# A dynamic convolution feeding a tanh-shrink MLP: the first x tile of a batch in one DMA, and another tap order for superblock 4

## The chip, the cores and the metric

The kernel runs on one core of one Trainium2 chip. The metric is the device time of one execution in microseconds (us); lower is better. The kernel before takes 751.6 us, the median of four runs (750.75 to 754.11). A core has five engines that run beside each other and wait for each other through semaphores: TensorE (PE, with its weight loads shown apart as PEld), VectorE (DVE), ScalarE (ACT), GpSimd (POOL) and SyncE (SP), which here only issues DMAs. Sixteen DMA engines move the data of all queues.

## What is computed

Eight batches of 4096 positions, 192 channels in 8 heads of 24. For each position and head a softmax over 7 taps gives weights; the output is the weighted sum of the 7 latest rows of x, zeros standing ahead of a batch's first row. That goes through a two-layer MLP with the activation h - tanh(h):

```python
def attn(x, weight_gen):
    w = softmax(weight_gen, axis=-1)              # [B, S, 8, 7]
    x_pad = concat([zeros(B, 6, 192), x], axis=1)
    out[b, s, h, g] = sum_k w[b, s, h, k] * x_pad[b, s + k, h, g]
    ...
h = out.reshape(32768, 192) @ w_in                # 192 x 2048
y = (h - tanh(h)) @ w_out                         # 2048 x 192
```

## The kernel before

The 32,768 tokens are cut into 32 superblocks of 1024. A batch has four, so superblocks 0, 4, 8, ... 28 are the first of a batch. On chip, each of the 128 partitions holds 8 consecutive tokens (J = 8). An x tile has 6 halo rows (the six tokens before the partition's own) and 8 rows: 14 rows of 192 floats, 10.5 KB per partition. Partition 0 of a batch's first tile has zeros in its halo rows.

For a superblock n the work passes through these stages.

1. SP loads the x tile (`load_x`, L110 to L150) and the tap weights (`load_wg`). Two x tiles exist. The load of tile n + 1 is tied by a dependency to the first product of superblock n (`x_after`, L280).
2. ScalarE takes the exponential of the weights, VectorE sums, inverts and scales.
3. `products` (from L229): GpSimd multiplies x rows by tap weights, giving seven bf16 product tensors: taps 0 to 3 in a tile `pa`, taps 4 to 6 in a tile `pb` that has a single buffer. For superblocks listed in HELP (4 to 31), one row of taps 0 and 1 is made by VectorE instead (L289). Product tensors are then partly summed by an accumulating DMA that GpSimd issues (`dma_sum`, L221). There are three ways: superblocks in PART add taps 2 and 3 onto 0 and 1 before the `pb` product is made, so five tensors remain; the others add the three of `pb` onto taps 0 to 2, so four remain; TWO_SUMS (13 on) add again, so two remain.
4. `conv_sums` (L338): PE transposes the remaining tensors against an identity matrix and sums them in PSUM; for each tensor 24 small matmuls, 16 for chunks 0 and 1 and 8 for chunk 2. ScalarE copies the result out as convT.
5. `gemm1` (L381) multiplies by one of 16 blocks (f) of w_in, ScalarE takes tanh (L394), VectorE subtracts (L395).
6. `out_pairs` (L417) multiplies by w_out, ScalarE copies out (L436), and SP stores (L440).

The order on each engine is the order in which the program is written. In the main loop, iteration n runs the 16 f steps of superblock n. In the same iteration stand: the products of superblock n + 2 (from f = 1, their second part at f = 3), the transposes of superblock n + 1 (chunks 0 and 1 at f = 13, chunk 2 at f = 14), the second matmul of superblock n - 1 and n spread as pairs over all f steps, and the loads of x tile n + 3 at f = 1 (at f = 9 in iteration 1). SP's queue therefore mixes x loads, weight loads and output stores in that order, and each waits its turn.

A batch's first x tile, except that of superblock 0, takes four DMAs: 112 partitions in full, rows without the halo for the first 16 partitions, the halo for partitions 1 to 15, and zeros for partition 0.

Of the kernel before, what the change touches and what calls it, by code (L numbers as in the profile page):

```python
# [16 lines left out]
def kernel(  # L17
# [8 lines left out]
    nc = tc.nc  # L26
# [15 lines left out]
    NFT = F // P  # L42
    NC = D // R
    KA, KH = 4, 2
    PART = (2, 3, 4)
    TWO_SUMS = (13, 14, 15, 16, 17, 18, 19, 20, 21, 22, 23, 24, 25, 26, 27, 28, 29, 30, 31)
    AHEAD = 4
    STORE_FIRST = 8
    EXTRA = (5, 9, 11, 13)
    HELP = (4, 5, 6, 7, 8, 9, 10, 11, 12, 13, 14, 15, 16, 17, 18, 19, 20, 21, 22, 23, 24, 25, 26, 27, 28, 29, 30, 31)  # L50
    HELP_AT = 3
    SCALE_TWICE = True
    assert S % TOK == 0 and D % R == 0 and F % P == 0
    assert NFT == 2 * J, "one token block of the second matmul per pair of f tiles"

# [14 lines left out]
    make_identity(nc, ident[:])  # L70

    obank = [psum_o.tile([P, 512], FP32, name=f"obank{i}", tag=f"obank{i}") for i in range(2)]
    zero = const.tile([1, D], FP32, name="zero")
    nc.vector.memzero(zero[:])
    once = const.tile([P, 1], FP32, name="once")
# [15 lines left out]
    last_conv = {}  # L91
    first_halo = {}
    x_after = {}

    def order(inst, other, reason):
        tc.add_manual_dep(
# [16 lines left out]
    def load_x(n, behind=None):  # L113
        b, s = divmod(n, NSB)
        s0 = s * TOK

        x_t = xpool.tile([P, HALO + J, D], FP32, name="x_t")

        def rows(p0, p1, r0=0, r1=HALO + J):
            first = x[0, 0:1]  # L120
            return nc.sync.dma_start(
                out=x_t[p0:p1, r0:r1, :],
                in_=bass.AP(
                    tensor=first.tensor,
                    offset=first.offset + (b * S + s0 + p0 * J - HALO + r0) * D,
                    ap=[[J * D, p1 - p0], [D, r1 - r0], [1, D]],
                ),
            )

        def no_halo():  # L130
            nc.sync.dma_start(
                out=x_t[0:1, 0:HALO, :],
                in_=zero[:].rearrange("o (h d) -> o h d", h=1).to_broadcast([1, HALO, D]),
            )


        if n == 0:
            rows(0, P, HALO, HALO + J)
            rows(16, P, 0, HALO)
            rows(1, 16, 0, HALO)  # L140
            no_halo()
        else:
            dma = rows(16 if s == 0 else 0, P)
            if behind is not None:
                order(dma, behind, "order of the loads")
            if s == 0:
                rows(0, 16, HALO)
                rows(1, 16, 0, HALO)
                no_halo()
        x_of[n] = x_t  # L150

    def softmax_exp(n):
# [75 lines left out]
    def products(n, taps=None, sums=None, hooks={}):  # L228

        x_t = x_of.pop(n)  # L230
        wsm, wsm_v, e_t, zr = wsm_of.pop(n)
        if e_t is not None:
            scale(nc.gpsimd, wsm[:], e_t, zr[:])

        pa = papool.tile([P, KA, J, D], BF16, name="pa")
        if n == 1:

            last = [opool.tile([P, 2, J, D], BF16, name="pb1", tag="out_sb") for _ in range(2)]
            home = [(pa, 0, KA), (last[0], KA, KA + 2), (last[1], KA + 2, K)]
        else:  # L240
            pb = pbpool.tile([P, K - KA, J, D], BF16, name="pb")
            home = [(pa, 0, KA), (pb, KA, K)]
        x_v = x_t[:]
        step = x_v.ap[0]

        def prod(k0, k1):
            for t, a, b in home:
                if a <= k0 and k1 <= b:
                    return t[:, k0 - a : k1 - a]

        def mul(eng, k0, k1, j0=0, j1=J):

            w = wsm_v if eng is nc.vector else wsm[:]
            nj = j1 - j0
            return eng.tensor_mul(  # L255
                prod(k0, k1)[:, :, j0:j1].rearrange("p k j (h g) -> p k (j h) g", h=H),
                bass.AP(
                    tensor=x_v.tensor,
                    offset=x_v.offset + (k0 + j0) * D,
                    ap=[step, [D, k1 - k0], [G, nj * H], [1, G]],  # L260
                ),
                w[:, j0:j1]
                .rearrange("p j h (k o) -> p k (j h) o", o=1)[:, k0:k1]
                .to_broadcast([P, k1 - k0, nj * H, G]),
            )

        def parts(*ks):
            return [[prod(k, k + 1)[:, 0] for k in ks]] * NC

        if taps is not None:  # L270
            for eng, k0, k1, j0, j1 in taps:
                m = mul(eng, k0, k1, j0, j1)
                if j1 == 1:
                    first_halo[0] = m
                if k0 in hooks:
                    hooks[k0]()
            prods_of[n] = parts(*sums)
            return

        x_after[n + 1] = mul(nc.gpsimd, 0, KH, 0, J - 1 if n in HELP else J)  # L280
        mul(nc.gpsimd, KH, KA)
        second_sum(n - 1)

        def rest(ph=None):
            if n in HELP:

                w = ph[:, 0, 0 : KH * H].rearrange("p (k h) -> p k h", k=KH)
                nc.vector.tensor_copy(w, wsm[:, J - 1].rearrange("p h k -> p k h")[:, 0:KH])
                nc.vector.tensor_mul(  # L289
                    pa[:, 0:KH, J - 1, :].rearrange("p k (h g) -> p k h g", h=H),  # L290
                    bass.AP(
                        tensor=x_v.tensor,
                        offset=x_v.offset + (J - 1) * D,
                        ap=[step, [D, KH], [G, H], [1, G]],
                    ),
                    w.rearrange("p k (h o) -> p k h o", o=1).to_broadcast([P, KH, H, G]),
                )
            if n in PART:
                dma_sum(pa[:, 0:2], pa[:, 2:4])
            mul(nc.gpsimd, KA, K)  # L300
            if n in PART:
                prods_of[n] = parts(4, 5, 6, 0, 1)
            else:
                dma_sum(pa[:, 0:3], pb[:, 0:3])
                if n in TWO_SUMS:
                    to_sum[n] = pa
                    prods_of[n] = parts(0, 1)
                else:
                    prods_of[n] = parts(3, 0, 1, 2)
                if n == NTOT - 1:  # L310
                    second_sum(n)

        return rest
# [62 lines left out]
    def gemm1(n, f):  # L376
        convT = conv_of[n]
        ph = psum_h.tile([P, 2, HT], FP32, name="ph", tag="ph")
        for c in range(NC):
            for r in range(2):  # L380
                nc.tensor.matmul(  # L381
                    ph[:, r, :],
                    lhsT=w_in[r * R : (r + 1) * R, c, f * P : (f + 1) * P],
                    rhs=convT[r * R : (r + 1) * R, c, :],
                    start=(c == 0),
                    stop=(c == NC - 1),
                )
        th = tpool.tile([P, TOK], FP32, name="th")
        ph_f = ph[:].rearrange("p r t -> p (r t)")
        gt = gpool.tile([P, TOK], BF16, name=f"gt{f}", tag=f"gt{f}")  # L390
        if n == 1 and f == 2:

            probe[0] = nc.scalar.activation(out=once[:], in_=ph_f[:, 0:1], func=ACT.Copy)
        last_act[0] = nc.scalar.activation(out=th[:], in_=ph_f, func=ACT.Tanh)  # L394
        last_sub[0] = nc.vector.tensor_sub(gt[:], ph_f, th[:])  # L395
        g_of.setdefault(n, []).append(gt)
        return ph

    LAST = (NTOT - 1) * J
    half = {}  # L400
# [162 lines left out]

    EARLY, THIRD = ((7, 3), (9, 1), (11, 7)), 13
    for f in range(NFT):
        gemm1(0, f)
        if f == 1:
            softmax_exp(3)
        if f == EARLY[0][0]:
            pcs = []  # L570
            sums = conv_sums(1, ((0, 1),), pcs, obank)
        for at, groups in EARLY:
            if f == at:
                some(sums, groups * PER)
        if f == EARLY[-1][0]:
            conv_out(1, ((0, 1),), pcs)
        if f == THIRD:
            pcs = []
            for _ in conv_sums(1, ((2,),), pcs, obank):
                pass  # L580
            conv_out(1, ((2,),), pcs)

    STEADY = dict(pairs=(5, 11, 0, 16, 4, 12, 6, 10, 0, 6, 10, 8, 8, 8, 8, 16), t1=(14, 8), t2=(13, 0), scale=14, sums=(1, 13))
    FIRST = dict(pairs=(4, 12, 0, 16, 1, 15, 0, 16, 0, 16, 0, 13, 3, 0, 16, 16), t1=(15, 2), t2=(11, 10), scale=15, sums=(1, 2, 3, 4, 8, 10))


    def transposes(n, chunks):
        pcs = []  # L590
# [16 lines left out]
    for n in range(1, NTOT):  # L607
        more = n < NTOT - 1
        finish = []
        plan = FIRST if n == 1 else STEADY  # L610

        soft = [m for m in (n + 3 if n <= AHEAD else n + 4,) if m < NTOT]
        for f in range(NFT):
# [42 lines left out]
            if f >= plan["scale"]:  # L656
                for scale_one in finish:
                    scale_one()
                finish = []
            out_pairs(plan["pairs"][f] - done)  # L660
            if f == (9 if n == 1 else 1) and n <= STORE_FIRST:
                loads(n)
# [36 lines left out]
```

## Time and profile before

| what | us |
|---|---|
| median of the runs | 751.6 |
| profiled execution, its run | 750.75 |
| its span in the profile | 749.0 |
| PE busy on the second matmul (L417) | 410.8 |
| PE busy on the first matmul (L381) | 419.9 |
| PE busy on transposes from pa / pb (L338) | 40.2 / 6.3 |
| one subtraction on DVE (L395) | 1.218 |
| one tanh on ACT (L394) | 1.026 |
| GpSimd product 128x4608 / 128x3072 / 128x2688 | 9.07 / 6.02 / 5.42 |
| sum pa<-pb, issue to landing (least, median, most) | 8.8, 9.5, 11.2 |
| x tile in one DMA, issue to landing, median | 7.7 |
| x tile's part of 112 partitions, the same | 9.2 |

Busy times of different engines lie beside each other, so they are not added. The matmuls of PE overlap each other as well. GpSimd's durations are means over the whole run[...]. The granted PE clock is full except at a few places. A superblock takes PE about 22.4 us in the first third and 21.8 us later, when fewer tensors are transposed.

### The profile page before, as it was taken

The numbers are of one execution on the slowest core, as the hardware profiler recorded it, in microseconds if no ns is written. First come the engines' busy times: TensorE is split into PE (matmuls) and PEld (weight loads), VectorE is DVE, ScalarE is ACT, GpSimd is POOL, SyncE is SP. The second block draws the span as 40 slices with busy tenths as digits, with TensorE's granted clock in tenths as the row PEclk, the third lists the DMA queues.
The fourth block names the chain that finished last, engine by engine and source line by source line (L and its number), as shares of the span: only waits on it lengthen the run. The fifth ranks groups of instructions, "written<-read, shape, count | busy, mean of one in ns | idle before, by whom it ended". The sixth has DMA issues, their size and how long they took to land.

```text
span 749.0 us, 30081 instructions
## 1 busy us (share of the span) xinstructions
PE 722.9 (97%) x13640; PEld 559.8 (75%) x13640; DVE 684.2 (91%) x711; ACT 639.9 (85%) x872; POOL 657.9 (88%) x158
## 2 busy tenths in 40 slices
PE   3899999999999989999999999999999999999997
PEld 2477777777777777777777777787777777877777
DVE  7999999989999979999999999999999999988893
ACT  4888888888888868888989989888998989888882
POOL 7999999999999999999999999999999999992000
PEclk9899999999999999999999999999999999999999
DMA  8926536865667659887779878787988877776112
GB/s 234 243 46 159 173 116 178 192 174 133 171 162 177 178 170 222 179 214 175 195 206 224 207 199 202 173 197 205 230 192 193 211 176 190 195 148 110 45 44 86
DMA packets 34464, 129.64 MB, mean 173 GB/s; under 512 B 4808, under 2 KB 9656, under 8 KB 30480
## 3 DMA queue, kind: packets, MB, share of 16 engines
q0 software_dynamic: 19296, 50.73, 39.4%
q1 hardware_dynamic: 15040, 77.00, 29.1%
q8 instruction: 106, 1.74, 0.9%
q14 instruction: 22, 0.18, 0.1%
HBM read 54.49 MB, written 25.17 MB: 106 GB/s over the span
## 4 chain that ended last, share of the span: by engine, by line
PE 93%; DVE 3%; issue 1%; DMA 1%; ACT 1%; DVEq 0%
PE obank L417 44%; PE ph L381 44%; PE pc L338 4%; PE po L460 1%; DVE gt L395 1%; DMA x_t<-in_x_dram 1%; ACT th L394 1%; DMA wg_t<-in_weight_gen_dram 0%; DVE pa L255 0%; DVE pb L255 0%; DVE wsm L214 0%; DVE zsum L168 0%; ACT wg_t L154 0%; DVE obank L196 0%; ACT convT L356 0%
## 5 line engine op out<-in xcount | busy, mean ns | idle before, releaser
L395 DVE TENSOR_TENSOR gt<-ph,th 128x1024 bf16<-128x1024 f32 x512 | 602.0, 1218 | 40.9 <-ACT th L394 27.8
L394 ACT ACTIVATE th<-ph 128x1024 f32<-128x1024 f32 x512 | 514.0, 1026 | 70.7 <-PE ph L381 62.4
L381 PE MATMUL ph<-convT,w_in 64*128 64x512 bf16 x3072 | 419.9, 379 | 5.0 <-DVE gt L395 3.5
L417 PEld LDWEIGHTS <-gt 64*128 64x128 bf16 x7936 | 357.7, 94 | 87.9 <-issue 14.0
L417 PE MATMUL obank<-w_out,gt 64*128 64x192 bf16 x7936 | 410.8, 243 | 6.0 <-issue 5.6
L255 POOL TENSOR_TENSOR pa<-x_t,wsm 128x3072 bf16<-128x3072 f32 (+2 forms) x63 | 341.6, 5655 | 0.2
L255 POOL TENSOR_TENSOR pb<-x_t,wsm 128x4608 bf16<-128x4608 f32 (+2 forms) x33 | 283.6, 8595 | 0.7 <-DMA x_t<-in_x_dram 0.4
L381 PEld LDWEIGHTS <-w_in 64*128 64x128 bf16 x3072 | 164.5, 95 | 79.8 <-issue 18.5
L436 ACT ACTIVATE out_sb<-obank 128x192 f32<-128x192 f32 x248 | 81.2, 328 | 15.4 <-PE obank L417 15.0
L364 ACT ACTIVATE convT<-pc 128x1024 bf16<-128x1024 f32 (+1 forms) x62 | 50.2, 811 | 1.2 <-PE pc L338 0.7
L221 POOL DMA_DIRECT2D pa<-pb x27 | 34.7, 1284 | 15.2 <-DVE pa L289 8.3
L338 PEld LDWEIGHTS <-pa 64*128 64x128 bf16 x2016 | 40.9, 100 | 7.2 <-POOL pa L255 1.1
L221 POOL DMA_DIRECT2D pa<-pa x22 | 35.4, 1607 | 8.7 <-DMA pa<-pb 7.8
L338 PE MATMUL pc<-ident,pa 64*128 64x64 bf16 x1920 | 40.2, 191 | 1.6 <-POOL pa L255 0.9
L168 DVE TENSOR_REDUCE zsum<-wg_t 128x32 f32<-128x224 f32 (+1 forms) x61 | 23.6, 387 | 3.0 <-ACT wg_t L154 3.0
L154 ACT ACTIVATE wg_t<-wg_t 128x448 f32<-128x448 f32 x32 | 18.2, 570 | 6.9 <-DMA wg_t<-in_weight_gen_dram 6.9
L214 DVE TENSOR_TENSOR wsm<-wg_t,pc 128x448 f32<-128x448 f32 x27 | 16.8, 621 | 3.0 <-DVE pc L183 0.5
L289 DVE TENSOR_TENSOR pa<-x_t,ph 128x384 bf16<-128x384 f32 x28 | 15.5, 554 | 1.2
L183 DVE RECIPROCAL pc<-zsum 128x64 f32<-128x64 f32 x27 | 14.9, 550 | 1.6 <-ACT convT L364 1.6
L338 PE MATMUL pc<-ident,pb 64*128 64x64 bf16 x288 | 6.3, 202 | 9.2 <-POOL pb L255 9.2
L338 PEld LDWEIGHTS <-pb 64*128 64x128 bf16 x360 | 7.7, 105 | 9.9 <-POOL pb L255 9.1
L460 PE MATMUL po<-w_out,gt 64*128 64x192 bf16 x256 | 11.2, 243 | 0.0
(27 smaller groups left out, 55.6 us busy)
## 6 DMA issues: line engine op xcount, KB each, us to landing
x_t<-in_x_dram SPq DMA_DIRECT2D x24, 1344.0 KB, 7.7
pa<-pb POOLq DMA_DIRECT2D x27, 1152.0 KB, 9.5
out_dram<-out_sb SPq DMA_DIRECT2D x31, 768.0 KB, 4.5
pa<-pa POOLq DMA_DIRECT2D x22, 768.0 KB, 7.5
x_t<-in_x_dram SPq DMA_DIRECT2D x7, 1176.0 KB, 9.2
wg_t<-in_weight_gen_dram SPq DMA_DIRECT2D x32, 224.0 KB, 7.3
x_t<-in_x_dram SPq DMA_DIRECT2D x1, 768.0 KB
w_out<-in_moe_w_out_dram POOLq DMA_DIRECT2D x1, 768.0 KB, 9.4
```

Source lines behind the costliest of these rows:

```text
L154: last_exp[0] = nc.scalar.activation(out=wg_t[:].rearrange("p j h k -> p (j h k)"), in_=wg_t[:].rearrange("p j h k -> p (j h k)"), func=AC ...
L168: nc.vector.reduce_sum(out=zsum_of[n][:, j0 * H : j1 * H], in_=e_of[n][:, j0:j1].rearrange("p j h k -> p (j h) k"), axis=AX.X,)
L221: return nc.gpsimd.dma_start(out=out.rearrange("p k j d -> p k (j d)"), in_=in_.rearrange("p k j d -> p k (j d)"), accum_op=mybir.AluOpTyp ...
L255: return eng.tensor_mul(prod(k0, k1)[:, :, j0:j1].rearrange("p k j (h g) -> p k (j h) g", h=H), bass.AP(tensor=x_v.tensor, offset=x_v.offs ...
L338: nc.tensor.matmul(pc[r][:, col : col + R] if home else pc[:, r, col : col + R], lhsT=prods[c][gi][r * R : (r + 1) * R, 2 * j : 2 * j + 2] ...
L364: last_conv[0] = nc.scalar.activation(out=out, in_=pc[:, :, 0:cols].rearrange("p r (cj t) -> p r cj t", t=R), func=ACT.Copy,)
L381: nc.tensor.matmul(ph[:, r, :], lhsT=w_in[r * R : (r + 1) * R, c, f * P : (f + 1) * P], rhs=convT[r * R : (r + 1) * R, c, :], start=(c == ...
L394: last_act[0] = nc.scalar.activation(out=th[:], in_=ph_f, func=ACT.Tanh)
L395: last_sub[0] = nc.vector.tensor_sub(gt[:], ph_f, th[:])
L417: mm = nc.tensor.matmul(po[:, 0:D], lhsT=g_of[n][f][r * R : (r + 1) * R, col : col + P], rhs=w_out[r * R : (r + 1) * R, f, :], start=(r == ...
L436: last_act[0] = nc.scalar.activation(out=out_sb[:, j, :], in_=po[:, 0:D], func=ACT.Copy)
L460: nc.tensor.matmul(po[:, r, 0:D], lhsT=g_of[n][f][r * R : (r + 1) * R, col : col + P], rhs=w_out[r * R : (r + 1) * R, f, :], start=(f == 0 ...
```

## The change

Superblock 4 leaves PART, so its taps 4 to 6 are summed by DMA onto taps 0 to 2. It is also in a new list, LAST_TAP: GpSimd makes taps 0 and 1, tap 2, then taps 4 to 6, issues the sum, and makes tap 3, which is not summed, last. PE's conv of superblock 4 now reads the four tensors 3, 0, 1, 2 in place of 4, 5, 6, 0, 1.

The first x tile of the batches 1 to 7 (superblocks 4, 8, ... 28) is loaded with one DMA over all partitions. For partition 0 this reads the last six rows of the previous batch into the halo. Zeros are written over them by a small DMA that is issued later, in iteration n - 3 at f = 8 (at f = 10 for superblock 4), and has to wait for the load to land.

Other new names (RELIEF, X_LATE, APART, gemm1_relieved) are empty or not reached.

```diff
-    PART = (2, 3, 4)
+    PART = (2, 3)
+    LAST_TAP = (4,)
+    X_LATE = ()
+    ZERO_AT = 8
...
-            dma = rows(16 if s == 0 else 0, P)
+            dma = rows(16 if s == 0 and ZERO_AT is None else 0, P)
             if behind is not None:
                 order(dma, behind, "order of the loads")
-            if s == 0:
+            if s == 0 and ZERO_AT is None:
                 rows(0, 16, HALO)
                 rows(1, 16, 0, HALO)
                 no_halo()
+            elif s == 0:
+                halo_of[n] = no_halo
...
-        x_after[n + 1] = mul(nc.gpsimd, 0, KH, 0, J - 1 if n in HELP else J)
-        mul(nc.gpsimd, KH, KA)
-        second_sum(n - 1)
+        first = mul(nc.gpsimd, 0, KH, 0, J - 1 if n in HELP else J)
+        if n in LAST_TAP:
+
+            x_after[n + 1] = mul(nc.gpsimd, KH, KA - 1)
+            second_sum(n - 1)
+        else:
+            mul(nc.gpsimd, KH, KA)
+            second_sum(n - 1)
+        if n not in LAST_TAP or n not in X_LATE:
+            x_after[n + 1] = first
...
                 dma_sum(pa[:, 0:3], pb[:, 0:3])
+                if n in LAST_TAP:
+                    mul(nc.gpsimd, KA - 1, KA)
...
+            if n + 3 in halo_of and f >= ZERO_AT:
+
+                halo_of.pop(n + 3)()
             out_pairs(plan["pairs"][f] - done)
```

More of the change, by code (lines that the diff above doesn't have):

```diff
@@ L50 @@
     HELP = (4, 5, 6, 7, 8, 9, 10, 11, 12, 13, 14, 15, 16, 17, 18, 19, 20, 21, 22, 23, 24, 25, 26, 27, 28, 29, 30, 31)
+    LAST_TAP = (4,)
+    X_LATE = ()
+    ZERO_AT = 8
     HELP_AT = 3
     SCALE_TWICE = True
+    RELIEF = ()
     assert S % TOK == 0 and D % R == 0 and F % P == 0
@@ L72 @@
     obank = [psum_o.tile([P, 512], FP32, name=f"obank{i}", tag=f"obank{i}") for i in range(2)]
+    if RELIEF:
+        minus = const.tile([P, P], FP32, name="minus")
+        nc.gpsimd.tensor_scalar_mul(minus[:], ident[:], -1.0)
     zero = const.tile([1, D], FP32, name="zero")
@@ L93 @@
     x_after = {}
+    halo_of = {}
     def order(inst, other, reason):
@@ L397, in gemm1, with gemm1_relieved, subtract, evict @@
         return ph
+    def gemm1_relieved(n, f):
+        convT = conv_of[n]
+        for c in range(NC):
+            for r in range(2):
+                nc.tensor.matmul(
+                    obank[r][:],
+                    lhsT=w_in[r * R : (r + 1) * R, c, f * P : (f + 1) * P],
+                    rhs=convT[r * R : (r + 1) * R, c, :],
+                    start=(c == 0),
+                    stop=(c == NC - 1),
+                )
+        th = tpool.tile([P, TOK], FP32, name="th")
+        gt = gpool.tile([P, TOK], BF16, name=f"gt{f}", tag=f"gt{f}")
+        for r in range(2):
+            nc.scalar.activation(out=th[:, r * HT : (r + 1) * HT], in_=obank[r][:], func=ACT.Tanh)
+        g_of.setdefault(n, []).append(gt)
+        def subtract():
+            for r in range(2):
+                nc.tensor.matmul(
+                    obank[r][:], lhsT=minus[:], rhs=th[:, r * HT : (r + 1) * HT], start=False, stop=True
+                )
+        def evict():
+            for r in range(2):
+                nc.scalar.activation(out=gt[:, r * HT : (r + 1) * HT], in_=obank[r][:], func=ACT.Copy)
+        return subtract, evict
     LAST = (NTOT - 1) * J
@@ L565 @@
     for f in range(NFT):
-        gemm1(0, f)
+        if f in RELIEF:
+            relieved = gemm1_relieved(0, f)
+        else:
+            gemm1(0, f)
+        for lag, step in ((1, 0), (2, 1)):
+            if f - lag in RELIEF:
+                relieved[step]()
         if f == 1:
@@ L581 @@
             conv_out(1, ((2,),), pcs)
+        out_pairs(dict(()).get(f, 0))
     STEADY = dict(pairs=(5, 11, 0, 16, 4, 12, 6, 10, 0, 6, 10, 8, 8, 8, 8, 16), t1=(14, 8), t2=(13, 0), scale=14, sums=(1, 13))
     FIRST = dict(pairs=(4, 12, 0, 16, 1, 15, 0, 16, 0, 16, 0, 13, 3, 0, 16, 16), t1=(15, 2), t2=(11, 10), scale=15, sums=(1, 2, 3, 4, 8, 10))
+    APART = dict(pairs=(4, 12, 0, 16, 0, 16, 4, 12, 0, 16, 4, 12, 0, 6, 10, 16), t1=(15, 5), t2=(10, 2), scale=15, sums=(7, 10))
+    APART_IN = ()
     def transposes(n, chunks):
@@ L609 @@
         finish = []
-        plan = FIRST if n == 1 else STEADY
+        plan = FIRST if n == 1 else APART if n in APART_IN else STEADY
         soft = [m for m in (n + 3 if n <= AHEAD else n + 4,) if m < NTOT]
```

## The prediction

> **What bounds the kernel now.** I read the page, then who waited for whom on PE after the start-up, then PE in order of time around its gaps, then DMA and clock in those stretches, last GpSimd around superblock 4.
>
> ```profile
> PE 722.9 (97%) x13640; PEld 559.8 (75%) x13640; DVE 684.2 (91%) x711; ACT 639.9 (85%) x872; POOL 657.9 (88%) x158
> ...
> q8 instruction: 106, 1.74, 0.9%
> ...
> PE 93%; DVE 3%; issue 1%; DMA 1%; ACT 1%; DVEq 0%
> ```
>
> The chain is TensorE work for 93%, so nothing counts unless it takes work from PE or idle time from it. The waits of PE between 40 and 740 us are a single row (waiting line, releaser, us in total, times, longest):
>
> ```profile
> PE obank L417 <- issue: 5.6, 5, 2.8
> ```
>
> So no GpSimd product, x load or sum holds PE up by name after the start-up: 5.6 us in five gaps for which no semaphore answers. The two large ones, in order of time (start, us, engine and line, idle before it):
>
> ```profile
> 149.55 0.74 PE L417 MATMUL obank<-w_out,gt 64*128 64x192 bf16 x13
> 152.15 0.32 PE L417 MATMUL obank<-w_out,gt 64*128 64x192 bf16 x3 [1.86 <-issue]
> ...
> 265.77 1.05 PE L417 MATMUL obank<-w_out,gt 64*128 64x192 bf16 x20
> 269.60 0.67 PE L417 MATMUL obank<-w_out,gt 64*128 64x192 bf16 x6 [2.79 <-issue]
> ```
>
> The stretches of the second (PE, PEld, DVE, ACT, POOL busy, then granted clock, DMA share, GB/s):
>
> ```profile
> 266.50:269.60 3.10, 0.32 (x8) 0.10 (x4) 2.11 (x3) 0.41 (x1) 3.10 (x2) 0.91 0.98 374
> 269.60:271.50 1.90, 1.90 (x15) 1.45 (x16) 0.00 (x0) 0.33 (x1) 1.90 (x2) 0.50 0.60 234
> ```
>
> PE stops in the middle of a group, and after the second gap it runs 1.9 us at clock 0.50. Counting PE's recorded instructions, the gaps stand before numbers 5313 and 9921, two smaller ones (0.46 at 318.7, 0.28 at 494.2) before 11713 and 18113: every distance is a multiple of 256. Queue q8 has 106 packets of 16.4 KB (1.74 MB / 106), and 27,280 matmuls and weight loads make 106.6 blocks of 256. They are instruction fetches that came late. From the packet records of q8, a fetch starts when PE enters a block, needs about 1 us, and PE goes on 1.5 us after its end (150.61 to 152.14; 268.11 to 269.60). A fetch asked for while a sum or load already stands in the DMA engines comes behind it: those of the two gaps were asked for at about 145 and 262 and served at 149.49 and 267.16. What stood before the first, and the same with an undivided x tile:
>
> ```profile
> DMA packets 376, 1.66 MB, mean 225 GB/s; under 512 B 85, under 2 KB 219, under 8 KB 263
> ...
> DMA packets 315, 1.65 MB, mean 285 GB/s; under 512 B 48, under 2 KB 176, under 8 KB 186
> ```
>
> 143.0 to 150.4 (x tile of superblock 8 in four pieces, its weights, the end of a sum) against 122.0 to 127.8 (superblock 7, one piece): equal bytes, 7.4 against 5.8 us. Last, GpSimd:
>
> ```profile
> 73.82 10.97 POOL L255 TENSOR_TENSOR pa<-x_t,wsm 128x2688 bf16<-128x2688 f32 x2
> 85.08 1.20 POOL L221 DMA_DIRECT2D pa<-pa  x1 [0.30 <-POOL pa L255]
> 85.86 8.80 POOL L255 TENSOR_TENSOR pb<-x_t,wsm 128x4608 bf16<-128x4608 f32 x1
> 94.17 10.96 POOL L255 TENSOR_TENSOR pa<-x_t,wsm 128x2688 bf16<-128x2688 f32 x2
> ```
>
> Superblocks 4 to 12 follow each other every 20.4 us without a wait, while PE takes 22.4: the sums' times do not depend on PE there.
>
> [...]
>
> **The change part by part.**
>
> *Fewer taps in the conv of superblock 4.* Five groups become four: 24 matmuls and 24 weight loads less. Chunks 0 and 1 took 101.47 to 102.63 (1.16 us, 80 matmuls), those of superblock 5 with four groups 124.81 to 125.74 (0.93); a third chunk in proportion 0.12. Gain 0.35 us, on PE.
>
> *GpSimd's order.* The first product stays (73.82 to 79.25). The second, 5.6 us, is cut into two of 2.9 (the row of 128x1536). The pb product moves ahead of the sum and would start at 82.2, but its single buffer is read by the conv of superblock 3 until 82.28: 82.4. It ends at 90.75, the sum is issued at 91.05, the last tap ends at 94.8. Superblock 5 starts at 94.82 instead of 94.17: all sums to superblock 12 come 0.65 us later. GpSimd has 2 us a superblock to spare, so this costs nothing by itself.
>
> *The new wait.* The sum of superblock 4 now carries three taps and is issued 6 us later. Such sums land 9.0 to 11.2 us after issue; with no x load beside it I take 9.3: 100.4. PE comes to that conv at 101.47, does the unsummed tap first (0.23) and needs the sum at 101.7: 1.3 us to spare, at worst (11.2) 0.6 us lost. Queued behind it are the matmuls of f = 13 and all after. I take nothing. Superblock 5 lands at 114.57 + 10.2 = 124.8, needed at 124.7: 0.1 us lost.
>
> *x tiles.* Seven tiles (4, 8, ... 28) lose two DMAs each; the issue falls from 2.0 to 0.33 us on SP. The zeros wait on SP for the tile: out_dram stores and the next x load stand behind them. Tile 4: landing 58.9 + 7.7 = 66.6, so the store of 64.98 goes at about 67.5; its buffer is wanted 20 us later. Tile 12: zeros at about 231, products at 238. Tiles 16 to 28: the zeros stand behind the store (319.56), products start at 325.43[...]. VectorE's own help product does not read the halo. Cost nothing, at worst 1 us on GpSimd, whose sums are 10 us early.
>
> *Instruction fetches.* The 48 missing instructions put every later block boundary 48 instructions later in the work, 0.35 to 1.8 us by where it falls. First gap: x tile 8 starts 0.65 later but is done about 1.6 us earlier; by superblock 7's fetch (3.4 to 4.7 us after the sum's end) it starts at 148.4 instead of 149.5, PE goes on at 151.0, where it would arrive at 150.3: 0.7 lost instead of 2.1. Then two fetches pin PE again: the one behind x tile 9 (PE resumes at 171.7, would reach this at 172.74 in the old timing: at most 1.0 us ahead), the one behind the sum of superblock 11 (248.8 against 249.36: at most 0.55). The one behind sum 12 lets PE go on at 270.25, with 48 more instructions done; the old kernel reached that point at 272.14. So 1.9 us ahead if the clock stays up, 0.6 if it halves again (the gap would be 2.84 us). I take 1.9, this includes all gains so far. Later, sums follow PE. The gaps of 318.7 and 494.2 lie behind the halo tiles 16 and 24 (308.40, 484.24), whose bursts shorten by 1.6 us: their 0.7 us of matmul time goes. New meetings: with boundaries 48 instructions on, those at 328.2, 503.6 and 678.9 fall 2.9 to 3.6 us after a sum's issue; a fetch is then done 10.8 us after it, the next boundary comes at 9.3 to 9.6: from nothing (a fetch just before the sum's packets, 1.85 us after issue) to 1.3 us each. I take nothing for them; all three are in the range.
>
> Sum: 1.9 + 0.7 = 2.6 us less than the profiled execution, whose run took 750.75 us around a span of 749.0. That run was the fastest of four; against the median of 751.6 I keep the difference: 749.0.
>
> **The rivals.** (a) *Faster, as above*: 749.0, chance 0.46; its own range 747.5 to 749.3. (b) *A gain that is pinned*: the clock halves again after 266 (1.3 us lost) and the new meetings cost about 1: 2.6 - 2.3 = 0.3 us, 751.3, within 0.3% (2.25 us, about what a measurement can tell from no change). For it: sums and loads keep their times whatever PE gains. Chance 0.38. (c) *Slower*: the shifted boundaries meet sums. Without the gain at 266, three new gaps of 1.3 us, 1.0 more behind sum 11, one of them long enough for the half clock (1.3): 6.2 - 1.4 (0.35 and the shorter burst) - 0.7 = 4.1, 755.7. It decides once more than 2.25 us of new gaps outlast the gains; against it, the four requests would all have to fall behind the sum's first packets. Chance 0.12. (d) *The second gap goes*: if PE is 1.9 us ahead at 240, the fetches of sums 11 and 12 are asked for before their packets: 2.8 + 1.3 + 2.1 + 0.35 less: 745.1; chance 0.04.
>
> **How the numbers follow.** Faster by over 0.3%: a and d, 0.50; within: 0.38; slower 0.12. The range 745.0 to 752.8 takes a, b, and d, and leaves out c and a tail of b.
>
> **What would show it.** Right: no PE gap of over 1 us near 150, sums from superblock 5 about 0.65 later, PE at the conv of superblock 12 ahead by 1 to 2 us, no gap at the halo tiles. Wrong: a wait of PE for the sum of superblock 4, GpSimd waiting for zeros, or new gaps at distances of 256 from 328, 504, 679. A time over 752.8 would say that the blocks' places, not the length of the bursts, decide.

## The result and the profile after

The changed kernel takes 748.12 us (median of 42 runs), the kernel before 751.31 us in the 63 runs measured beside it: a ratio of 0.995, 95% interval 0.9939 to 0.9961. That is 3.2 us less where 2.6 was forecast. The profiled executions stand 750.75 to 747.22 us, their spans 749.0 to 745.5.

The page of the changed kernel. Labels have moved: L357 is the conv, L400 the first matmul, L466 the second, L231 the summing DMA, L265 the products.

```profile
PE 720.4 (97%) x13616; PEld 555.8 (75%) x13616; DVE 684.2 (92%) x711; ACT 639.2 (86%) x872; POOL 658.1 (88%) x159
...
q8 instruction: 106, 1.74, 0.9%
...
PE 87%; DVE 4%; POOL 3%; DMA 2%; issue 2%; ACT 1%; SPq 0%; DVEq 0%; POOLq 0%
```

Still PE, still 106 instruction fetches. What has changed is in the waits of PE between 40 and 740 us (waiting line, releaser, us in total, times, longest):

```profile
PE obank L466 <- issue: 2.4, 4, 1.2
PE pc L357 <- issue: 1.3, 1, 1.3
PE pc L357 <- DMA pa<-pb: 0.6, 1, 0.6
PE ph L400 <- DVE pa L306: 0.2, 1, 0.2
```

The 5.6 us of unexplained stops have become 3.7, and a wait for a sum has come in. The gap near 150 us is gone. In order of time around the three large ones that are there now (start, us, engine and line, idle before it):

```profile
124.16 0.42 PE L357 MATMUL pc<-ident,pa 64*128 64x64 bf16 x16
125.19 0.88 PE L357 MATMUL pc<-ident,pa 64*128 64x64 bf16 x48 [0.61 <-DMA pa<-pb]
...
266.07 0.57 PE L466 MATMUL obank<-w_out,gt 64*128 64x192 bf16 x9
267.84 0.24 PE L466 MATMUL obank<-w_out,gt 64*128 64x192 bf16 x1 [1.19 <-issue]
...
286.84 0.48 PE L357 MATMUL pc<-ident,pa 64*128 64x64 bf16 x21
288.67 0.33 PE L357 MATMUL pc<-ident,pa 64*128 64x64 bf16 x11 [1.35 <-issue]
```

The stop at 266 us is 1.2 us where it was 2.8 (idle time), and the clock behind it stays whole, where it fell to 0.50 before. The stretches there (busy of PE, PEld, DVE, ACT, POOL, then granted clock, DMA share, GB/s):

```profile
266.00:268.00 2.00, 0.81 (x16) 0.57 (x13) 1.81 (x3) 1.02 (x1) 2.00 (x1) 1.00 1.08 284
268.00:270.00 2.00, 2.00 (x35) 1.71 (x33) 0.75 (x2) 1.24 (x2) 2.00 (x2) 1.00 1.00 391
```

The stop of 1.35 us at 287 is new: the kernel before ran 282 to 292 us without one. To see where time came from and went back, I follow PE through the same work in both traces, by the number of PE instructions done (less the 48 that are missing after superblock 4):

| same point of the work, at us before | after minus before | what lies between |
|---|---|---|
| 99.1 | -0.30 | start |
| 147.9 | +0.15 | fewer taps, then 0.80 lost at the conv of superblock 5 |
| 153.4 | -1.88 | first gap gone |
| 264.6 | -1.56 | small losses, no stop over 0.5 |
| 282.2 | -4.55 | second gap 1.43 in place of 3.03 from start to start, no half clock |
| 312.8 | -3.02 | new gap of 1.54 at 287 |
| 386.8 | -2.47 | gaps of 0.57 at 331 and 0.91 at 379 |
| 744.2 | -3.17 | nothing large |

So the change has gained 4.55 us by 282 us, and 1.4 of it is given back.

GpSimd around superblock 4 (same columns as PE):

```profile
73.67 8.24 POOL L265 TENSOR_TENSOR pa<-x_t,wsm 128x2688 bf16<-128x2688 f32 x2
82.14 8.35 POOL L265 TENSOR_TENSOR pb<-x_t,wsm 128x4608 bf16<-128x4608 f32 x1 [0.22 <-PE pc L357]
90.78 1.28 POOL L231 DMA_DIRECT2D pa<-pb  x1 [0.30 <-POOL pb L265]
91.60 13.86 POOL L265 TENSOR_TENSOR pa<-x_t,wsm 128x1536 bf16<-128x1536 f32 x3
```

The last row runs the unsummed tap of superblock 4 into the two products of superblock 5. The sum of superblock 4, issued at 90.78, had no one waiting for it at 101.4.

Last, the DMA view of 138 to 155 us, x tile 8 among it (queue: packets, MB, share of 16 engines), before:

```profile
DMA packets 669, 2.58 MB, mean 152 GB/s; under 512 B 85, under 2 KB 219, under 8 KB 555
...
q1 hardware_dynamic: 346, 1.61, 36.5%
```

and after:

```profile
DMA packets 633, 2.62 MB, mean 154 GB/s; under 512 B 54, under 2 KB 188, under 8 KB 502
...
q1 hardware_dynamic: 300, 1.61, 23.7%
```

The load queue moves the same 1.61 MB in both (the x tile and the tap weights); 46 packets fewer take a third less time of the DMA engines: 6.2 us of all sixteen against 4.0 (share times 17 us).

### The profile page after: what moved, and what is told of

It is laid out like the page before. It is cut to its first block, busy times and chain, and to the rows that moved or that the text cites. A ratio compares the mean times of both kernels' runs of the same rounds, so it can differ in the third digit from the quotient of the medians.

```text
span 745.5 us, 30018 instructions
## 1 busy us (share of the span) xinstructions
PE 720.4 (97%) x13616; PEld 555.8 (75%) x13616; DVE 684.2 (92%) x711; ACT 639.2 (86%) x872; POOL 658.1 (88%) x159
## 3 DMA queue, kind: packets, MB, share of 16 engines
q8 instruction: 106, 1.74, 0.9%
## 4 chain that ended last, share of the span: by engine, by line
PE 87%; DVE 4%; POOL 3%; DMA 2%; issue 2%; ACT 1%; SPq 0%; DVEq 0%; POOLq 0%
PE ph L400 41%; PE obank L466 41%; PE pc L357 4%; DVE gt L414 2%; POOL pb L265 2%; DMA pa<-pb 1%; PE po L509 1%; POOL pa L265 1%; DMA wg_t<-in_weight_gen_dram 1%; DVE pa L265 1%; ACT th L413 1%; DVE zsum L178 0%; ACT convT L375 0%; SPq L129 0%; DVE obank L206 0%
## 5 line engine op out<-in xcount | busy, mean ns | idle before, releaser
L400 PE MATMUL ph<-convT,w_in 64*128 64x512 bf16 x3072 | 417.4, 378 | 5.8 <-DVE gt L414 4.0
L466 PEld LDWEIGHTS <-gt 64*128 64x128 bf16 x7936 | 355.7, 94 | 83.3 <-issue 7.8
L466 PE MATMUL obank<-w_out,gt 64*128 64x192 bf16 x7936 | 408.1, 243 | 2.6 <-issue 2.4
L265 POOL TENSOR_TENSOR pa<-x_t,wsm 128x2688 bf16<-128x2688 f32 (+2 forms) x64 | 341.9, 5579 | 0.2
L265 POOL TENSOR_TENSOR pb<-x_t,wsm 128x4608 bf16<-128x4608 f32 (+2 forms) x33 | 283.3, 8587 | 0.9 <-ACT wsm L216 0.5
L400 PEld LDWEIGHTS <-w_in 64*128 64x128 bf16 x3072 | 161.2, 94 | 83.1 <-issue 17.9
L357 PEld LDWEIGHTS <-pa 64*128 64x128 bf16 x2064 | 41.8, 100 | 9.6 <-issue 1.8
L231 POOL DMA_DIRECT2D pa<-pb x28 | 36.0, 1284 | 12.0 <-POOL pb L265 9.1
L357 PE MATMUL pc<-ident,pa 64*128 64x64 bf16 x1968 | 40.9, 191 | 3.9 <-issue 1.3
L231 POOL DMA_DIRECT2D pa<-pa x21 | 34.6, 1650 | 9.2 <-DMA pa<-pb 8.6
L193 DVE RECIPROCAL pc<-zsum 128x64 f32<-128x64 f32 x27 | 14.9, 551 | 1.0 <-ACT convT L383 1.0
L357 PE MATMUL pc<-ident,pb 64*128 64x64 bf16 x216 | 4.9, 206 | 9.0 <-POOL pb L265 9.0
L357 PEld LDWEIGHTS <-pb 64*128 64x128 bf16 x288 | 6.3, 107 | 9.5 <-POOL pb L265 9.0
```

What stands on the lines that cost most here:

```text
L231: return nc.gpsimd.dma_start(out=out.rearrange("p k j d -> p k (j d)"), in_=in_.rearrange("p k j d -> p k (j d)"), accum_op=mybir.AluOpTyp ...
L265: return eng.tensor_mul(prod(k0, k1)[:, :, j0:j1].rearrange("p k j (h g) -> p k (j h) g", h=H), bass.AP(tensor=x_v.tensor, offset=x_v.offs ...
L357: nc.tensor.matmul(pc[r][:, col : col + R] if home else pc[:, r, col : col + R], lhsT=prods[c][gi][r * R : (r + 1) * R, 2 * j : 2 * j + 2] ...
L400: nc.tensor.matmul(ph[:, r, :], lhsT=w_in[r * R : (r + 1) * R, c, f * P : (f + 1) * P], rhs=convT[r * R : (r + 1) * R, c, :], start=(c == ...
L466: mm = nc.tensor.matmul(po[:, 0:D], lhsT=g_of[n][f][r * R : (r + 1) * R, col : col + P], rhs=w_out[r * R : (r + 1) * R, f, :], start=(r == ...
```

## The experiments

Three theories. **Burst**: the single x load shortens the burst in front of the fetch, removes the first gap, and the lead gained there softens the second. **Place**: it is the 48 missing instructions, which move every block boundary. **Taps**: the order of the taps in superblock 4 matters by itself. In the expectations below, "theory F" is the first of these (late instruction fetches set the gain), "rival W" says that only PE's own work counts, and "rival D" that the x loads count.

**1. Each part alone.** Starting from the changed kernel, one run leaves the x loads in pieces, the other leaves superblock 4 as it was.

```diff
-    ZERO_AT = 8
+    ZERO_AT = None          # e1_taps_only
...
-    PART = (2, 3)
-    LAST_TAP = (4,)
+    PART = (2, 3, 4)        # e2_one_dma_only
+    LAST_TAP = ()
```

> The tap part of the change alone; first tiles of a batch still come in four DMAs. Theory F (late instruction fetches set the gain): 0.35 us of matmuls less, block boundaries 48 instructions later as in the changed kernel, but long bursts behind the first tiles; the gap near 150 us keeps some 1 to 2 us, the one near 266 us may shrink. 0.5 to 2.5 us less than before, ratio 0.997 to 0.999. Rival W (only the work counts): 0.35 us less, ratio 0.9995. Rival D (the x loads are the gain): no difference.

> The single x load with late zeros alone; superblock 4 as before, so all block boundaries stay at the instructions of the kernel before. Theory F: the gap near 150 us falls from 2.1 to 0.5 to 1 us, PE is then pinned by the late fetch near 266 us, which stays; 0.5 to 1.5 us less, ratio 0.998 to 0.9995. Rival D: nearly the whole gain, 3 us or more less, ratio 0.996 or below. Rival W: no difference.

Taps alone: 749.0 us, ratio 0.9975 (0.9961 to 0.9988), as expected. One DMA alone: 747.66 us, 0.9956 (0.9935 to 0.9977), as good as both together. Here the expectation failed: theory F had the fetch near 266 us pin PE and gave 0.998 to 0.9995, and the time is the one that it left to rival D. The parts alone give 0.25% and 0.44%, together 0.69%, and the change 0.5%; with intervals of 0.13, 0.21 and 0.11 to either side, the runs do not show whether the parts add. With the taps alone the first gap stays, PE in order of time:

```profile
149.99 0.48 PE L357 MATMUL pc<-ident,pa 64*128 64x64 bf16 x21
151.89 0.33 PE L357 MATMUL pc<-ident,pa 64*128 64x64 bf16 x11 [1.42 <-issue]
```

With one DMA alone PE does not stop at all between 140 and 300 us; its waits from 40 to 740 are

```profile
PE obank L466 <- issue: 2.7, 7, 0.7
PE obank L466 <- ACT th L413: 1.1, 1, 1.1
PE pc L357 <- issue: 0.6, 1, 0.6
PE ph L400 <- issue: 0.4, 1, 0.4
```

It has all block boundaries where the kernel before has them, so place is not what removes the first gap; the burst is. The other traces agree. Five kernels load tile 8 in pieces, and four of them stop at a block boundary there for 1.6 to 2.3 us from start to start; the fifth, with 104 idle matmuls (below), comes there 4.6 us late and does not. Of the eight kernels that load it in one DMA, only the one with split sums (experiment 7) stops there, for 0.88. One DMA alone is 7.0 us ahead of the kernel before at 282 us, and gives 4.4 of that back: six gaps of 0.57 to 1.47 between 332 and 442 us, each 768 instructions, three blocks, after the last.

**2. Place alone.** Idle matmuls ahead of the first conv of the kernel before move its boundaries: 104 (with their weight loads 208 instructions) put them where the changed kernel has them, 128 are a whole block. Nothing of the computation is left out; the matmuls' results are not used.

```diff
+    fill = psum_h.tile([P, 2, HT], FP32, name="fill", tag="ph")
+    for _ in range(104):    # 128 in e4_before_fill128
+        nc.tensor.matmul(fill[:, 0, 0:R], lhsT=ident[0:R, :], rhs=ident[0:R, 0:R], start=True, stop=True)
```

> The kernel before, with 104 idle matmuls on an identity (208 instructions, results unused) ahead of PE's first work, where PE waits for the first products. They put every block boundary 48 instructions later in the work, as in the changed kernel, and change nothing else after the start. Theory F: the gaps after 40 us stand elsewhere than in the kernel before, at the work of the changed kernel's boundaries, and their sum differs by 1 us or more; the time moves by 1 to 4 us against the run with 128 idle matmuls. Rivals W and D: the same gaps, the same time as with 128.

> The kernel before with 128 idle matmuls (256 instructions, one whole block) ahead of PE's first work: every boundary falls on the same piece of work as before. Theory F: gaps of about 2 us near 150 and 3 us near 266 us at the same matmuls as in the kernel before, time within 0.7 us of it, apart from what the idle matmuls do to the start. Rival: if the gaps are chance, they stand elsewhere in this profile.

With 104: 751.61 us, 0.9991 (0.9972 to 1.0011). With 128: 752.39 us, 1.0019 (0.9993 to 1.0046). In time, place alone gives nothing that these runs can tell from no change; the 1 to 4 us that were expected between the two are not seen. In the traces it moves the gaps: with a whole block the first stands before number 5569, which is 5313 + 256, the same work as before; with 104 it is gone from there, and others stand at 104.7 (3.29), 225.7 (1.31) and 246.7 us (2.62), all at distances of 256 from the old numbers. That the stops are block boundaries is shown by this. How long a stop lasts is not fixed by the boundary: with a whole block the stop of 3.03 us at 266 has become 1.10 (at 272), and two of 1.9 us, at 223 and 246 us, stand where the kernel before has none. That was not expected; PE had come 1.4 us later out of the first stop and the slow clock behind it. The run with a whole block shows also what a stop can cost beside itself, PE in order of time and the stretches:

```profile
149.41 0.74 PE L417 MATMUL obank<-w_out,gt 64*128 64x192 bf16 x13
152.24 0.47 PE L417 MATMUL obank<-w_out,gt 64*128 64x192 bf16 x3 [2.09 <-issue]
```

```profile
150.00:152.00 2.00, 0.15 (x4) 0.00 (x0) 1.23 (x1) 0.65 (x1) 2.00 (x1) 1.00 0.02 6
152.00:154.00 2.00, 1.76 (x39) 1.54 (x40) 0.00 (x0) 0.73 (x2) 2.00 (x1) 0.53 0.04 8
```

Almost the stop of the kernel before (1.86), but this time the clock halved; over these 2 us it is 0.53 in the mean.

**3. Place under the change.** The same idle matmuls in the changed kernel: 24 (48 instructions) put its boundaries back to those of before, 64 half a block on; and 64 with one DMA alone.

> The changed kernel with 24 idle matmuls (48 instructions) ahead of PE's first work: the block boundaries return to the pieces of work where the kernel before has them, the loads and taps stay changed. If the place of the boundaries was a part of the gain, it goes: ratio 0.997 or above. If the short bursts are the gain and the place only says where the rest of the gaps stand: ratio 0.994 to 0.996, gaps at other matmuls than in the changed kernel.

> The same with 64 idle matmuls (128 instructions, half a block). Short bursts as the gain: ratio 0.992 to 0.997, the spread being what the place of the boundaries can do; place as the gain: outside that. Gaps again only at multiples of 256 from each other.

> The single x load with late zeros alone (taps as before) with 64 idle matmuls. Together with the runs without and the changed kernel: if all versions with the single load lie within 0.2% of each other, neither taps nor places matter, ratio 0.994 to 0.997; otherwise the place does.

With 24: 749.86 us, 0.9983 (0.997 to 0.9996). With 64: 747.54 us, 0.9948 (0.9934 to 0.9962). With 64 and one DMA alone: 747.83 us, 0.9945 (0.9924 to 0.9965). Two of three places keep the gain. With 24 about 2.5 us of it are lost (0.9983 against 0.995), which is where the expectation put place as a part of the gain; and so not all versions with the single load lie within 0.2% of each other. In the profile with 24, 1.2 us of this are there at 40 us, ahead of the loads and taps that the change touches (one execution was profiled, so whether every one starts like this is open); after 300 us it has the gaps of the run with one DMA alone, at the same numbers (12481, 13249, 14017, 16321), and it is 2.4 us behind the changed kernel at the end. So place alone does not make the gain (experiment 2), but a bad place can go with the loss of two thirds of it. About half of this loss may come from where earlier requests meet other bursts; the other half is not explained.

The sum of the stops is no measure of the time by itself either. The profile with 64 and one DMA alone has 6.2 us of them, more than the 5.6 of the kernel before, in a span of 748.0 us; none lies near 150 us, and none is followed by the half clock. (Its run took 749.77 us, 1.9 above the median.)

**4. The zeros.** One DMA alone, with the zeros written right behind the load rather than some f steps later.

```diff
-                halo_of[n] = no_halo
+                no_halo()
```

> Single x load for the first tiles, tap part as before, but the zeros stand right behind the load on SP instead of at f = 8. SP then stands still until the tile has landed (7 to 8 us), with the weight load and the store behind it. Theory F: the bursts are as short as with late zeros, so the gap near 150 us is gone and the time is that of the version with late zeros within 0.15%, ratio 0.995 to 0.997. Rival: the late place of the zeros carries the gain; ratio 0.999 or above.

747.08 us, 0.9946 (0.9925 to 0.9967): inside the interval of the kernel without this edit. The late place of the zeros earns nothing here, and costs nothing.

**5. Pieces everywhere.** The kernel before with each x tile in pieces, to see the price of pieces when there is more of it.

```diff
-            dma = rows(16 if s == 0 else 0, P)
+            dma = rows(16, P)
...
+            rows(0, 16, HALO)
...
+            else:
+                rows(0, 16, 0, HALO)
```

> The opposite dose: the kernel before with every x tile in three pieces (112 partitions, and rows and halo of the first 16 apart), so that each load makes a longer burst in the DMA engines, not one in four. Theory F: late fetches behind more x loads, gaps of 1 to 2 us at several more block boundaries; 2 to 8 us slower than before, ratio 1.003 to 1.011. Rival D (a tile's arrival counts): GpSimd never waited for x, so no difference.

775.35 us, 1.0316 (1.0275 to 1.0357), almost three times the loss that was expected at most. Its waits of PE begin

```profile
PE obank L419 <- issue: 9.9, 11, 3.6
PE ph L383 <- issue: 4.4, 3, 2.1
```

and GpSimd waits for no x tile after 30 us. So beyond the start-up pieces do not hurt by a late tile: the late fetches are 14.9 us of PE (9.9 + 4.4, and 0.6 at the conv), against 5.6 before. Of the 19.2 us between the profiled spans (768.2 and 749.0) that is 9.3; another 4.4 are there at 23 us, in the start-up; the rest was not placed. The profiled run is the fastest of four (769.97 us), so some 5 us of the median's loss are in no trace.

**6. The unsummed tap's place.** Superblock 4 summed over three taps as in the change, but with tap 3 made where the other superblocks make it, ahead of the sum.

```diff
-    LAST_TAP = (4,)
+    LAST_TAP = ()
```

> The changed kernel with superblock 4 still in three tap sums but its unsummed tap made in the usual place, before the pb product; the sum is issued 2.9 us later, near 93.7 us, and lands near 103. PE wants it at 101.4. Prediction's sum: PE waits 1.5 to 2 us for the sum of superblock 4; that time is kept or lost again at the next late fetch, 0 to 2 us slower than the changed kernel, ratio to before 0.995 to 0.998. Rival: the sum is not needed so early, the order is of no account: no wait, ratio as the changed kernel, 0.995.

747.93 us, 0.9965 (0.9953 to 0.9976). Now PE does wait for the sum of superblock 4:

```profile
101.59 0.41 PE L357 MATMUL pc<-ident,pa 64*128 64x64 bf16 x16
103.09 0.88 PE L357 MATMUL pc<-ident,pa 64*128 64x64 bf16 x48 [1.09 <-DMA pa<-pb]
```

The order in LAST_TAP does what it can do, it takes away 1.09 us here; but the end hardly moves (0.9965 against 0.995, intervals overlapping). In the traces this kernel is 0.9 us behind the changed one at 148 us and 0.3 us at the end: stops that follow take the difference back.

**7. Shorter sums.** If a fetch waits for a whole sum, half a sum should hold it less long: the sums of superblocks 5 to 12 are split, taps 4 and 5 first, tap 6 after its own product.

```diff
+                mul(nc.gpsimd, KA, KA + 2)
+                dma_sum(pa[:, 0:2], pb[:, 0:2])
+                mul(nc.gpsimd, KA + 2, K)
+                dma_sum(pa[:, 2:3], pb[:, 2:3])
```

> The changed kernel with the pb product and its sum of superblocks 5 to 12 cut in two (taps 4 and 5, then 6): two bursts of about 4.7 and 2.3 us with GpSimd's third product between, in place of one of 7. Costs GpSimd 1.1 us more a superblock, of the 2 us it has to spare there. Theory F: a fetch waits 4.7 us at most, so PE has no gap of over 1 us between 130 and 280 us; 0.5 to 3 us faster than the changed kernel, ratio to before 0.991 to 0.994. Rival: the gaps only move; ratio 0.995. If GpSimd gets late, PE waits for sums and it is slower.

755.86 us, 1.0071 (1.0053 to 1.009): slower, where faster was expected. What was expected of the fetches did come: between 130 and 280 us no stop at a block boundary is over 0.88 us. What was wrong is that GpSimd could spare the time. Its second half of a superblock:

```profile
236.63 5.92 POOL L266 TENSOR_TENSOR pb<-x_t,wsm 128x3072 bf16<-128x3072 f32 x1
242.85 1.22 POOL L232 DMA_DIRECT2D pa<-pb  x1 [0.30 <-POOL pb L266]
243.62 3.38 POOL L266 TENSOR_TENSOR pb<-x_t,wsm 128x1536 bf16<-128x1536 f32 x1
247.30 0.90 POOL L232 DMA_DIRECT2D pa<-pb  x1 [0.30 <-POOL pb L266]
```

One superblock to the next is 21.77 us (225.53 to 247.30) where it was 20.4. GpSimd is busy 88% of the span, and the lead that it had built up by superblock 12 is gone: the sum of superblock 13 is issued at 289.12 us, in the changed kernel at 278.74. PE at superblock 13:

```profile
306.69 0.83 PE L408 MATMUL ph<-convT,w_in 64*128 64x512 bf16 x6
311.37 1.04 PE L365 MATMUL pc<-ident,pa 64*128 64x64 bf16 x32 [3.86 <-DMA pa<-pa]
```

Of the 8.6 us between the ends of these two traces this stop is 4.2. After 313 us another 3.8 are lost, most of it in four stops of 0.8 to 1.6 us between 363 and 451 us.

## Why the prediction was right, and where its steps were off

**The bound and the mechanism.** Right, and shown: the gaps sit on block boundaries (experiment 2), and the single load removes the first (experiment 1). That the total came so near, 3.2 us for 2.6, is in part luck, as the terms show.

**Taps.** Forecast -0.35 us. PE's lead goes from 0.30 to 0.65 us over the three chunks of that conv: 0.35, as forecast. The gap of 0.80 at the next conv takes it back, and more.

**GpSimd and sum 4.** Right: issue forecast at 91.05, measured 90.78; landing at 100.4, measured 100.29; the sum was forecast 1.3 us ahead of PE, and no wait is seen. The sums of superblocks 5 to 12 come 0.13 to 0.32 us later, where 0.65 was forecast. "Superblock 5 lands at 114.57 + 10.2": it was issued at 114.05, and PE goes on with it at 125.19, 11.1 us later. The term "0.1 us lost" measured 0.80. Neither part alone shows this wait, and neither do the changed kernels with 24 and 64 idle matmuls, which have both parts; why the sum took 11.1 us here is open.

**x tiles and zeros.** Right: GpSimd waits for no zeros (its only waits between 40 and 740 us are for sums, products and VectorE, and 0.2 us for a buffer that PE reads), and their place is of no account (experiment 4). No view shows when they land. The burst at tile 8 was forecast 1.6 us shorter; by the packets of the load queue it lasts 143.3 to 149.3 in place of 143.1 to 150.3, 1.2 us shorter.

**First gap.** Forecast 2.1 to 0.7; it went to nothing. The fetch was served at 148.17 (forecast 148.4, before 149.49), and PE came to its boundary only at 150.65, since it had lost 0.8 at the conv of superblock 5. That loss is not what saved it: one DMA alone has no such loss and no gap, its fetch being served at 146.88 and its boundary reached at 149.42.

**Where the steps failed.** "Then two fetches pin PE again": at most 1.0 us ahead behind x tile 9, at most 0.55 behind sum 11, and 2.84 us of gap left at 266. Nothing of this happened: PE kept 1.56 us up to 264 us, and the gap was 1.43. I had held the end of a fetch fixed to the sum in front of it. The runs show that it moves with the moment at which it is asked for. The records do not hold the request itself; the moment at which PE enters the block before stands for it. (In the kernel before, every fetch after 40 us starts between 0.6 us before that moment and 5.0 us after it.) Six kernels, one and the same block at superblock 12, from the trace's packets of q8; the sum's first packets move 1.85 us after its issue:

| kernel | asked for, us after the sum's issue | served, us after the sum's issue | gap of PE at 266, us |
|---|---|---|---|
| one DMA alone | 1.41 | 3.00 | none |
| one DMA, zeros at once | 1.74 | 4.35 | 0.51 |
| after | 2.62 | 7.24 | 1.43 |
| tap 3 first | 2.81 | 7.24 | 1.30 |
| before | 4.16 | 9.17 | 3.03 |
| taps alone | 4.16 | 8.95 | 1.58 |

Asking 1.5 us earlier (4.16 to 2.62) goes with being served 1.9 us earlier, and another 1.2 us (2.62 to 1.41), ahead of the sum's packets, with another 4.2. (The last row arrives at its boundary 1.1 us later than "before", 48 instructions on, so its gap is smaller at nearly the same time of service.)

The sums of the other superblocks show the same. In the twelve traces without split sums, 47 fetches were asked for 0 to 1.4 us after the issue of a three-tap sum, and they started 0.3 us later (median; 1.24 at most). Another 138 were asked for 3.3 to 6 us after it, and they started 2.8 to 5.2 us later (median 4.0).

In what order the DMA engines take what stands before them is not shown. In the changed kernel the fetch moves at 265.56, while packets of the sum still start. In the kernel before it moves at 267.16, 0.9 us after the first packet of an x load (266.27) that was issued at 264.29, 2.1 us after PE had entered the block. Of the 1.98 us from issue to first packet of that load only about 1 us is waiting: with no sum beside it an x load also takes 0.99 us (79.24 to 80.23).

So here a lead was not pinned, it grew: that is rival (d), which had "asked for before their packets" for its condition and 0.04 for its chance. With one DMA alone the condition was met (1.64 us after sum 11, 1.41 after sum 12) and the gap is gone, though the time is 747.66 us and not 745.1. In the changed kernel it was not met (2.96 and 2.62), and half of the gap went all the same.

**What took it back.** "New meetings ... I take nothing for them." PE is 3 to 4.5 us earlier, the sums of superblocks 13 to 16 only 0.9 to 2.7, so it meets new ones: 1.54 at 287, where the fetch was asked for at 283.29, 4.56 us after sum 13's issue, and served at 286.46; then 0.57 and 0.91. None over 0.5 us lies at 504 or 679 us; the one at 331 stands where 328 was named. That is rival (b)'s cost of "about 1", at 3.0 us in place of 1. The gaps at 318.7 and 494.2 went, as forecast, but not shown to go for the reason given, shorter bursts of tiles 16 and 24: with the taps alone, where these tiles still come in pieces, the first went too (0.09 us) and the second shrank from 0.52 to 0.37, and with one DMA alone 0.48 us of the first stays. The total came out near because two terms were off in opposite directions: 4.55 us gained by 282 where 1.9 was forecast (2.65 more), and behind it 1.38 given back where 0.7 more was to be gained (2.1 less). Rival (c), slower, asked for more new gaps than gains; the gains were larger.

**What stays open.** Why the meetings come back once per superblock in some places of the boundaries and not in others. Three blocks take PE 21.1 us late in the kernel (109.9 us for 4,000 instructions), and the sums of superblocks 13, 14 and 15 are issued every 21.68 us, so a meeting can return until the boundary has slid away from it. That fits the run of gaps at distances of 768, but it was not tried by itself.

## What to carry to other kernels

When PE stops in the middle of a group with no releaser, number the stops by instruction: distances that are multiples of the fetch block (256 instructions here) point to late fetches, and what to shorten is the DMA burst in front of them, not an engine (one DMA alone: 0.9956). Price a lead of PE by when its next requests are made, not by the old ends of what it waits for (asked for 1.5 us earlier, the fetch at 266 was served 1.9 us earlier); and expect part of it to be given back where the earlier requests meet other bursts (1.4 of 4.55 us here). An edit that lets off the bursts by adding work to an engine at 88% can cost more than the stops (the split sums: 755.86 us, against 748.12 without them).

## What the runs showed of the hardware

- A DMA cut by partitions costs more of the engines' time at equal bytes: 6.2 against 4.0 us for 1.61 MB (6.6 with the taps alone, 4.1 with one DMA alone), and cutting every tile costs 3.2% of the whole.
- The half clock after a stop is not a matter of its length alone. Idle times of 2.79 us (before: clock 0.50 from 269.6 to 271.5), 2.09 (whole block of idle matmuls: 0.53 from 152 to 154) and 2.07 (pieces everywhere, at 551 us: 0.98 in the mean of 470 to 560) were followed by it. One of 1.86 in the kernel before was not (1.00 from 152 to 154), and neither were 2.42 (104 idle matmuls, at 247 us), 2.23 and even 3.56 (pieces everywhere, at 140 and 91 us: 1.00 in all stretches from 80 to 165). In the clock records of the kernel before, the half-clock spells ahead of the end last 3.413 us each, and they start at 16.48, 23.31 and 269.07 us, 2 and 72 times that length apart. Counted in stretches of this length, between 40 and 740 us of all thirteen traces, each of the five stretches with 1.97 us or more of idle PE was followed by the half clock, and none of the others was, the longest idle being 1.94. The 3.56 us fell half into one stretch and half into the next (1.94 and 1.61). This is a count and no limit: in the start-up of the changed kernel a stretch with 1.90 us (from 12.41 on) was followed by the half clock.
- After a late fetch PE goes on 2.2 to 2.5 us after the fetch's first packet, in all five of the kernels above that stop at 266 (267.84 after 265.56; 269.60 after 267.16).
